# From layer 1 to layer 2 of a fused attention and two-layer MoE kernel: order of the last choice of expert, block 0's rows, ranks and the third block

## The chip, the cores and the metric

One NeuronCore of a Trainium2 chip runs the whole program. The metric is device time in microseconds, the median over runs; lower is better. Engines are named as the profile names them: PE (TensorE, matmul), DVE (VectorE), ACT (ScalarE), POOL (GpSimd) and SP (SyncE, which issues most transfers).

## The reference

Pooled attention over 8 x 8 heads feeds two mixture-of-experts layers on 4608 tokens of width 512, with 8 experts of hidden width 1024, one expert a token. Layer 2 leaves a token as it is unless its skip score is positive.

```python
# layer 1
e_idx = np.argmax(x @ w_gate + modality_bias[modality_id], axis=1)
for e in range(8):
    m = e_idx == e
    out[m] = gate_w[m, None] * (np.maximum(x[m] @ w1[e], 0) @ w2[e])
# layer 2, on layer 1's output x
do = x @ w_skip > 0
e2 = np.argmax(x[do] @ w_gate2, axis=1)
...
out[do] = x[do] + y
```

## The kernel before, in words

**Blocks.** Each layer sorts its tokens by expert into blocks of 256 slots (two tiles of 128). A block is gathered by row number into `xg` (two buffers, by the block's parity), transposed on PE (`xT`), split into a high and a low half (`xh`, `xl`), multiplied with `w1` in eight steps (`gemm1`, line 1388), and each tile then with `w2` in eight steps of three matmuls (`gemm2`, line 1448). Every product is three matmuls: high by high, high by low, low by high. `hh` and `hl` are the halves of the hidden layer; `split_w1` and `split_w2` make the weights' halves (ACT the high, DVE or POOL the low one).

**Routing of layer 2** runs beside layer 1. For every block that layer 1 has finished, DVE makes the logits (line 1728), and `picks` (line 1647) makes two steps on POOL: `first` (lines 1659 to 1674; with one maximum on DVE, `rt_mx`) and `second` (lines 1676 to 1689; with one maximum on DVE, `rt_my`), which ends with the running counts `rti`, the block's write to DRAM (`x2s`, through SP) and a scatter to the output. `rank` (line 1700) then counts with two matmuls R (lines 1707 and 1708) each token's place among its expert's: R goes to a PSUM slot with the tag `m`, of which there is one and which the routing's other counts use too; DVE reads R (`rt_rk`, line 1712). `route_places` writes four tables `OB` on POOL.

**The way over.** How many blocks layer 1 has is known only at run time; `rec` (line 1974) branches, and behind its last block runs `first2(n)` (line 1593). Block 0 of layer 2 has been gathered early, into the buffer of parity `n % 2`, and its first product runs as `gemm1(n, f)`. `epilogue2` (line 1631) adds block 0's rows from `xg[0]`; for an odd `n` they are gathered once more, into `xg[0]`. Each `gather` is two DMAs on POOL's queue, one a tile. Here `n` is 19. `first2` issues its gathers ahead of its loop; in the loop the last block's `first` and `second` come at steps 2 and 4, the rank of the block before at step 6, and the last rank at step 1 of block 0's `gemm2`, where `route` (line 1777) is begun at step 2.

**Background.** `route` is a queue of generators. Every step of `gemm2`, and in `second` twice every step of `gemm1`, calls `tick`, which runs `pace` of their steps (lines 673 to 680). The route's last steps write `gidx` (line 1046), the row numbers of all blocks of layer 2.

**Block 1.** `Layer.second` (line 1782) runs block 1's `gemm1` and first `gemm2`, then flushes the route, gathers block 2, and gives block 2's `w1` halves and transposes out over block 1's second `gemm2`. PSUM slots: three for `gemm1`, two for `gemm2`, two with the tag `tp` for transposes (`ps_t`, line 1357), one `m`.

An engine takes its instructions in program order, so an instruction that waits holds up all behind it on that engine.

Of the kernel before, what the change touches and what calls it, by code (L numbers as in the profile page):

```python
# [24 lines left out]
E = 8  # L25
# [681 lines left out]
T = 256  # L707
# [463 lines left out]
class Moe:  # L1171
# [421 lines left out]
    def first2(self, n):  # L1593

        nc, g = self.nc, self.g
        ranks = self.ranks
        self.ranks = []
        todo = [x for x in self.todo[:-11]]
        first, second = self.picks(n - 1)
        self.todo = []  # L1600
        nc.vector.tensor_copy(self.gate0, self.gate[n % 2])
        if n % 2:
            self.gather(g.r2.gidx0, 0, 0, g.x2s[0:16 * T, :])
        self.gather(g.r2.gidx0, 2, 1, g.x2s[0:16 * T, :])
        late = self.late_logits(n - 1)
        for f in range(8):
            self.gemm1(n, f)
            for x in todo[2 * f:2 * f + 2 if f < 7 else None]:
                x[2]()
            if f in (0, 2):  # L1610
                next(late)
            if f == 2:
                first()
            if f > 1:
                self.split_w2(f - 2)
            if f == 4:
                second()
            if f == 6:
                self.rank_all(ranks)
        for f in range(6, 8):  # L1620
            self.split_w2(f)
        self.gates1(1, self.sp)
        self.gemm2(0, 0, self.epilogue2, {1: self.rank_all, 2: self.L2.route,
                                          3: lambda: self.xT(1, 0, self.ps_t("ps_x")),
                                          5: lambda: self.xT(1, 1, self.ps_t("ps_x"))})
        self.gates2(1, self.sp)
        self.gemm2(0, 1, self.epilogue2)
        self.scatter(n - 1, 1)
        self.L2.second()

    def epilogue2(self, i, t, ps):
        nc, g = self.nc, self.g
# [11 lines left out]
            out=self.out, out_offset=bass.IndirectOffsetOnAxis(ap=si, axis=0), in_=o,  # L1644
            in_offset=None, bounds_check=NT - 1, oob_is_err=False)

    def picks(self, i):

        nc, g = self.nc, self.g
        P, V = nc.gpsimd, nc.vector  # L1650
# [25 lines left out]
        def second():  # L1676
            eq, val = st["eq"], st["val"]
            my = tile("rt_my")
            V.tensor_reduce(out=my, in_=eq, axis=AX.X, op=ALU.max)
            P.tensor_tensor(eq, eq, bc(my), ALU.subtract)  # L1680
            P.tensor_scalar(M, eq, 0.0, None, ALU.is_ge)
            P.tensor_tensor(M, M, bc(val), ALU.mult)
            for c in range(2):
                P.tensor_tensor(r2.carry, r2.carry, M[:, c, :], ALU.add)
                P.tensor_copy(I[:, c, :], r2.carry)
            nc.sync.dma_start(
                out=g.x2s[T * i:T * i + T, :].rearrange("(t p) w -> p t w", t=2), in_=x2)
            self.scatter(i, 0)
            self.ranks.append(i)

        return first, second

    def scatter(self, i, t):
        self.nc.gpsimd.indirect_dma_start(  # L1694
# [5 lines left out]
    def rank(self, i):  # L1700

        nc, g, r2 = self.nc, self.g, self.g.r2
        V = nc.vector
        M, I = r2.M[:, 2 * i:2 * i + 2, :], self.rti[i % 2]
        B = r2.BB[:, 2 * i:2 * i + 2]
        R = self.pp.tile([128, 2, E], F32, tag="m", name="R")
        nc.tensor.matmul(R, lhsT=g.trim, rhs=M, start=True, stop=False)
        nc.tensor.matmul(R, lhsT=g.ones, rhs=I, start=False, stop=True)
        rk = self.sp.tile([128, 2, E], F32, tag="rt_rk", name="rt_rk")
        ra = self.sp.tile([128, 2], F32, tag="rt_ra", name="rt_ra")  # L1710
        ri = self.sp.tile([128, 2], I32, tag="rt_ri", name="rt_ri")
        V.tensor_tensor(rk, M, R, ALU.mult)
        V.tensor_reduce(out=ra, in_=rk, axis=AX.X, op=ALU.add)
        V.tensor_copy(ri, ra)
        V.tensor_scalar(ri, ri, 127, None, ALU.bitwise_and)
        V.tensor_copy(B, ri)
        nc.gpsimd.tensor_tensor(r2.RH[:, 2 * i:2 * i + 2], ra, B, ALU.subtract)
        for _ in route_places(self.tc, g, r2, 2 * i, 2, nc.gpsimd):
            pass
# [33 lines left out]
class Layer:  # L1753
# [28 lines left out]
    def second(self):  # L1782

        m, g = self.m, self.m.g
        tc, r = m.tc, self.r
        bg = g.bg
        for f in range(8):
            m.gemm1(1, f)
# [2 lines left out]
        m.gemm2(1, 0, self.epilogue)  # L1791
        bg.flush()
        self.gather(2)
        if self.n == 1:
            self.gather(3)
        if self.n == 2:
            m.nc.vector.tensor_scalar(g.empty, r.tokf, BIG - 1.5, BIG, ALU.is_gt, ALU.mult)
        self.load_regs(2)
        self.load_w1(2)
        self.load_w2(2)  # L1800
        if self.n == 1:
            m.load_split(2)
            m.split_w1_if(range(8))
            m.drip(7)
        else:
            for f in range(4):
                m.split_w1(f, m.nc.gpsimd if f == 3 else None)

        def next_x(t):
            m.xT(2, t, m.ps_t("ps_x"))  # L1810
            if self.n == 2:
                m.split_w1(4 + 2 * t)
                m.split_w1(5 + 2 * t, m.nc.gpsimd)

        m.gemm2(1, 1, self.epilogue, {3: lambda: next_x(0), 5: lambda: next_x(1),
                                      6: lambda: m.gates1(2, m.sp)})
        m.gates2(2, m.sp)
        if self.n == 1:
            m.drip(5)

    def body(self, i):
        m = self.m
# [220 lines left out]
```

## Time and profile before

| | |
|---|---|
| median of 3 runs | 971.68 us (969.25 to 972.96) |
| profiled execution | 972.93 us |
| its span | 971.2 us, mean granted clock 0.964 |
| PE busy | 908.2 us (94%) |
| DVE busy | 694.7 us (72%) |
| POOL busy | 518.1 us (53%) |
| ACT busy | 372.0 us (38%) |

All times of the trace count from the start of the span. A share of busy time is an average over stages; what a stage costs is read from the gaps of PE in it and from what ended each. "Granted clock" is the share of PE's full 2.4 GHz: 1.00, or 0.50 for 1.2 GHz; a stretch that holds both shows a value between. Matmul rows overlap: the start of one to the start of the next is what one costs.

### The profile page before, as it was taken

How to read it: one execution, taken by the hardware profiler on the slowest of the kernel's cores; microseconds unless marked ns; L12 is line 12 of the kernel's file. 1: busy time of each engine (PE TensorE's matmuls, PEld its weight loads, DVE VectorE, ACT ScalarE, POOL GpSimd, SP SyncE). 2: the span in 40 equal slices, each digit the busy share in tenths (PEclk: the TensorE clock that was granted, in tenths of full speed). 3: DMA queues.
4: the chain of work that ended last, by engine and by line, in shares of the span. 5: the costliest groups of instructions: out<-in, count | busy, mean ns of one | idle time of the engine just before them, and what ended most of it. 6: DMA issues, size and time to landing. Idle time of an engine off the chain costs nothing. (4 is left out here: it accounts for less than half of the span.)

```text
span 971.2 us, 19083 instructions
## 1 busy us (share of the span) xinstructions
PE 908.2 (94%) x6205; PEld 813.5 (84%) x6205; DVE 694.7 (72%) x1843; ACT 372.0 (38%) x733; POOL 518.1 (53%) x765
## 2 busy tenths in 40 slices
PE   6899999899999999998999989999598999999994
PEld 5798898888899999987999879979586988878983
DVE  4376786776787788889777897868574667567564
ACT  2465565544122222251222512213212556565454
POOL 4745698303246647666765566565543444444443
PEclk7799999999999999999999999999988999999998
DMA  9997975523211211431224412237203764571341
GB/s 229 223 250 215 243 203 165 160 83 95 84 65 57 94 37 64 145 145 64 83 78 151 153 66 71 72 92 240 80 36 100 237 217 143 183 251 35 114 150 41
DMA packets 87386, 126.57 MB, mean 130 GB/s; under 512 B 14361, under 2 KB 51225, under 8 KB 87115
## 3 DMA queue, kind: packets, MB, share of 16 engines
q1 hardware_dynamic: 75386, 96.68, 32.7%
q0 software_dynamic: 10640, 28.12, 9.3%
q8 instruction: 62, 1.02, 0.4%
q14 instruction: 82, 0.66, 0.2%
q10 hardware_dynamic: 1216, 0.08, 0.1%
HBM read 184.72 MB, written 39.50 MB: 231 GB/s over the span
## 5 line engine op out<-in xcount | busy, mean ns | idle before, releaser
L1402 PE MATMUL ps_g<-xh,w1h 128*128 128x256 f32 x896 | 256.6, 286 | 2.3 <-DVE hl L1407 1.6
L1402 PE MATMUL ps_g<-xl,w1h 128*128 128x256 f32 x896 | 253.9, 283 | 2.6 <-DVE xl L1354 2.6
L1402 PE MATMUL ps_g<-xh,w1l 128*128 128x256 f32 x896 | 253.2, 283 | 0.0
L1728 DVE CUSTOM_DVE_ANT_0 junk<-x,W 128x512 bf16<-128x512 f32 x333 | 234.5, 704 | 19.5 <-DVEq L1332 6.2
L1455 PE MATMUL ps_g<-w2h,hh 128*128 128x512 f32 x464 | 193.6, 417 | 1.0 <-DVE rs_v L1043 0.5
L1455 PE MATMUL ps_g<-w2h,hl 128*128 128x512 f32 x464 | 186.8, 403 | 6.1 <-DVE hl L1407 6.1
L1455 PE MATMUL ps_g<-w2l,hh 128*128 128x512 f32 x464 | 186.1, 401 | 0.0
L1402 PEld LDWEIGHTS ps_g<-xh,w1h 128*128 128x128 f32 x896 | 169.9, 190 | 8.4 <-DVE hl L1407 2.0
L1402 PEld LDWEIGHTS ps_g<-xl,w1h 128*128 128x128 f32 x896 | 169.5, 189 | 4.6 <-DVE xl L1354 3.6
L1402 PEld LDWEIGHTS ps_g<-xh,w1l 128*128 128x128 f32 x896 | 169.5, 189 | 0.0
L1406 ACT ACTIVATE hh<-ps_g 128x512 fp32r<-128x512 f32 (+1 forms) x116 | 67.6, 583 | 249.5 <-PE ps_g L1402 247.1
L906 POOL TENSOR_SCALAR OB<-iota,BB,pay 128x128 bf16<-128x128 bf16 x126 | 111.9, 896 | 22.8 <-DVE BB L894 18.8
L1407 DVE SCALAR_TENSOR_TENSOR hl<-ps_g,hh 128x512 fp32r<-128x512 f32 (+1 forms) x116 | 77.6, 669 | 57.6 <-ACT hh L1406 37.9
L1455 PEld LDWEIGHTS ps_g<-w2h,hl 128*128 128x128 f32 x464 | 89.1, 192 | 30.1 <-DVE hl L1407 7.6
L1455 PEld LDWEIGHTS ps_g<-w2h,hh 128*128 128x128 f32 x464 | 89.5, 193 | 19.6 <-ACT hh L1424 1.8
L1455 PEld LDWEIGHTS ps_g<-w2l,hh 128*128 128x128 f32 x464 | 89.8, 194 | 16.9
L1322 POOL TENSOR_TENSOR w1l<-w1r,w1h 128x512 fp32r<-128x512 f32 x40 | 51.6, 1309 | 61.8 <-ACT w1h L1321 61.5
L1344 DVE TENSOR_TENSOR w2l<-w2r,w2h 128x512 fp32r<-128x512 f32 x112 | 75.2, 709 | 8.8 <-ACT w2h L1343 5.7
L1694 POOL DMA_INDIRECT out_dram<-x,dsi x38 | 47.2, 1242 | 48.1 <-DMA out_dram<-x,dsi 13.4
L1321 ACT CAST w1h<-w1r 128x512 fp32r<-128x512 f32 x120 | 68.3, 619 | 0.5 <-ACT hh L1406 0.5
L1343 ACT CAST w2h<-w2r 128x512 fp32r<-128x512 f32 x112 | 63.9, 616 | 4.1 <-DVE gidxf L1046 2.5
L1643 POOL DMA_INDIRECT out_dram<-o,o2i x21 | 25.6, 1217 | 74.7 <-DVE o2i L1642 30.7
(291 smaller groups left out, 1422.9 us busy)
## 6 DMA issues: line engine op xcount, KB each, us to landing
w1r<-in_moe_w_dram SPq DMA_DIRECT2D x128, 512.0 KB
w2r<-in_moe_w_dram SPq DMA_DIRECT2D x128, 512.0 KB
x2s<-x SPq DMA_DIRECT2D x19, 522.0 KB
v<-in_v_dram SPq DMA_DIRECT2D x48, 192.0 KB
xd<-x SPq DMA_DIRECT2D x16, 520.0 KB
q_sb<-in_q_dram SPq DMA_DIRECT2D x16, 512.0 KB
kt<-in_k_dram SPq DMA_DIRECT2D x32, 144.0 KB
x2s<-OBx SPq DMA_DIRECT2D x16, 261.0 KB
```

What stands on the lines that cost most here:

```text
L906: e.tensor_scalar(g.ob(c)[:, i, :], g.iota, r.BB[:, c:c + 1], r.pay[:, i, c:c + 1], ALU.is_equal, ALU.mult)
L1321: self.nc.scalar.copy(self.w1h[f], raw)
L1322: (eng or self.nc.vector).tensor_tensor(self.w1l[f], raw, self.w1h[f].bitcast(F32), ALU.subtract)
L1343: self.nc.scalar.copy(self.w2h[f], raw)
L1344: (eng or self.nc.vector).tensor_tensor(self.w2l[f], raw, self.w2h[f].bitcast(F32), ALU.subtract)
L1402: nc.tensor.matmul(out, lhsT=a[f][:, k, :], rhs=b[:, k, :], start=(n == 0), stop=(n == 11))
L1406: nc.scalar.activation(out=hh, in_=whole, func=ACTF.Relu)
L1407: nc.vector.scalar_tensor_tensor(hl, in0=whole, scalar=0.0, in1=hh.bitcast(F32), op0=ALU.max, op1=ALU.subtract)
L1455: nc.tensor.matmul(ps, lhsT=a[f][:, tt], rhs=b[f], start=(n == 0), stop=(n == 23))
L1643: nc.gpsimd.indirect_dma_start(out=self.out, out_offset=bass.IndirectOffsetOnAxis(ap=si, axis=0), in_=o, in_offset=None, bounds_check=NT - ...
L1694: self.nc.gpsimd.indirect_dma_start(out=self.out, out_offset=bass.IndirectOffsetOnAxis(ap=self.dsi[i % 2][:, t:t + 1], axis=0), in_=self.x ...
L1728: self.nc.vector.tensor_tensor_reduce(out=self.junk, in0=self.x2[i % 2][:, t, 0:DM], in1=self.W9[:, e, :], scale=1.0, scalar=0.0, op0=ALU. ...
```

## The change

- `picks` can give a third part, `third` (write to `x2s`, scatter, note for the rank). In `first2` the gathers ahead of the loop go: the one of block 0 is replaced by a copy on ACT at step 1, the one of block 1 stands at step 4, between `second` and `third`.
- In block 0's first `gemm2` the background's pace is 3 instead of 2, block 1's transposes stand at steps 4 and 6 instead of 3 and 5, and `gates1` of block 1 at step 7 instead of ahead of the product.
- `rank` puts R into a transposes' slot (`tp`, two of them) instead of `m`, in every block.
- Layer 2's block 1 runs in a function of its own, `second2`: it gathers block 2 as soon as the route is done, within block 1's `gemm1`; the `w1` halves stand at steps 4 to 7 of the first `gemm2`, the transposes at steps 1 and 3 of the second.

```diff
--- before.py
+++ after.py
@@ -1596,12 +1596,9 @@
         ranks = self.ranks
         self.ranks = []
         todo = [x for x in self.todo[:-11]]
-        first, second = self.picks(n - 1)
+        first, second, third = self.picks(n - 1, False)
         self.todo = []
         nc.vector.tensor_copy(self.gate0, self.gate[n % 2])
-        if n % 2:
-            self.gather(g.r2.gidx0, 0, 0, g.x2s[0:16 * T, :])
-        self.gather(g.r2.gidx0, 2, 1, g.x2s[0:16 * T, :])
         late = self.late_logits(n - 1)
         for f in range(8):
             self.gemm1(n, f)
@@ -1609,24 +1606,29 @@
                 x[2]()
             if f in (0, 2):
                 next(late)
+            if f == 1 and n % 2:
+                nc.scalar.copy(self.xg[0], self.xg[1])
             if f == 2:
                 first()
             if f > 1:
                 self.split_w2(f - 2)
             if f == 4:
                 second()
+                self.gather(g.r2.gidx0, 2, 1, g.x2s[0:16 * T, :])
+                third()
             if f == 6:
                 self.rank_all(ranks)
         for f in range(6, 8):
             self.split_w2(f)
-        self.gates1(1, self.sp)
+        g.bg.pace = 3
         self.gemm2(0, 0, self.epilogue2, {1: self.rank_all, 2: self.L2.route,
-                                          3: lambda: self.xT(1, 0, self.ps_t("ps_x")),
-                                          5: lambda: self.xT(1, 1, self.ps_t("ps_x"))})
+                                          4: lambda: self.xT(1, 0, self.ps_t("ps_x")),
+                                          6: lambda: self.xT(1, 1, self.ps_t("ps_x")),
+                                          7: lambda: self.gates1(1, self.sp)})
         self.gates2(1, self.sp)
         self.gemm2(0, 1, self.epilogue2)
         self.scatter(n - 1, 1)
-        self.L2.second()
+        self.L2.second2()
 
     def epilogue2(self, i, t, ps):
         nc, g = self.nc, self.g
@@ -1644,7 +1646,7 @@
             out=self.out, out_offset=bass.IndirectOffsetOnAxis(ap=si, axis=0), in_=o,
             in_offset=None, bounds_check=NT - 1, oob_is_err=False)
 
-    def picks(self, i):
+    def picks(self, i, whole=True):
 
         nc, g = self.nc, self.g
         P, V = nc.gpsimd, nc.vector
@@ -1683,12 +1685,16 @@
             for c in range(2):
                 P.tensor_tensor(r2.carry, r2.carry, M[:, c, :], ALU.add)
                 P.tensor_copy(I[:, c, :], r2.carry)
+            if whole:
+                third()
+
+        def third():
             nc.sync.dma_start(
                 out=g.x2s[T * i:T * i + T, :].rearrange("(t p) w -> p t w", t=2), in_=x2)
             self.scatter(i, 0)
             self.ranks.append(i)
 
-        return first, second
+        return (first, second) if whole else (first, second, third)
 
     def scatter(self, i, t):
         self.nc.gpsimd.indirect_dma_start(
@@ -1703,7 +1709,7 @@
         V = nc.vector
         M, I = r2.M[:, 2 * i:2 * i + 2, :], self.rti[i % 2]
         B = r2.BB[:, 2 * i:2 * i + 2]
-        R = self.pp.tile([128, 2, E], F32, tag="m", name="R")
+        R = self.ps_t("R2")[:, 0, 0:2 * E].rearrange("p (c e) -> p c e", e=E)
         nc.tensor.matmul(R, lhsT=g.trim, rhs=M, start=True, stop=False)
         nc.tensor.matmul(R, lhsT=g.ones, rhs=I, start=False, stop=True)
         rk = self.sp.tile([128, 2, E], F32, tag="rt_rk", name="rt_rk")
@@ -1782,7 +1788,6 @@
     def second(self):
 
         m, g = self.m, self.m.g
-        tc, r = m.tc, self.r
         bg = g.bg
         for f in range(8):
             m.gemm1(1, f)
@@ -1791,32 +1796,57 @@
         m.gemm2(1, 0, self.epilogue)
         bg.flush()
         self.gather(2)
-        if self.n == 1:
-            self.gather(3)
-        if self.n == 2:
-            m.nc.vector.tensor_scalar(g.empty, r.tokf, BIG - 1.5, BIG, ALU.is_gt, ALU.mult)
+        self.gather(3)
         self.load_regs(2)
         self.load_w1(2)
         self.load_w2(2)
-        if self.n == 1:
-            m.load_split(2)
-            m.split_w1_if(range(8))
-            m.drip(7)
-        else:
-            for f in range(4):
-                m.split_w1(f, m.nc.gpsimd if f == 3 else None)
+        m.load_split(2)
+        m.split_w1_if(range(8))
+        m.drip(7)
+        m.gemm2(1, 1, self.epilogue, {3: lambda: m.xT(2, 0, m.ps_t("ps_x")),
+                                      5: lambda: m.xT(2, 1, m.ps_t("ps_x")),
+                                      6: lambda: m.gates1(2, m.sp)})
+        m.gates2(2, m.sp)
+        m.drip(5)
+
+    def second2(self):
+
+        m, g = self.m, self.m.g
+        r, bg, pool = self.r, g.bg, m.nc.gpsimd
+        ready = []
+
+        def begin():
+            if ready or bg.q:
+                return
+            ready.append(True)
+            self.gather(2)
+            self.load_regs(2)
+            self.load_w1(2)
+            self.load_w2(2)
+            m.nc.vector.tensor_scalar(g.empty, r.tokf, BIG - 1.5, BIG, ALU.is_gt, ALU.mult)
+
+        for f in range(8):
+            m.gemm1(1, f)
+            bg.tick()
+            bg.tick()
+            begin()
+        bg.flush()
+        begin()
+        bg.pace = 2
+
+        def split(f):
+            return lambda: m.split_w1(f, pool if f in (3, 7) else None)
+
+        m.gemm2(1, 0, self.epilogue, {4 + f: split(f) for f in range(4)})
 
         def next_x(t):
             m.xT(2, t, m.ps_t("ps_x"))
-            if self.n == 2:
-                m.split_w1(4 + 2 * t)
-                m.split_w1(5 + 2 * t, m.nc.gpsimd)
-
-        m.gemm2(1, 1, self.epilogue, {3: lambda: next_x(0), 5: lambda: next_x(1),
-                                      6: lambda: m.gates1(2, m.sp)})
+            split(4 + 2 * t)()
+            split(5 + 2 * t)()
+
+        m.gemm2(1, 1, self.epilogue, {1: lambda: next_x(0), 3: lambda: next_x(1),
+                                      5: lambda: m.gates1(2, m.sp)})
         m.gates2(2, m.sp)
-        if self.n == 1:
-            m.drip(5)
 
     def body(self, i):
         m = self.m
```

## Rows read from the trace of the kernel before

**Rows 1.** Timeline of PE around both gaps: start, us, engine, line, out<-in, count [idle<-releaser].
```profile
694.12 0.39 PE L1455 MATMUL ps_g<-w2l,hh 128*128 128x512 f32 x1
694.36 0.39 PE L1455 MATMUL ps_g<-w2h,hl 128*128 128x512 f32 x1
...
703.23 0.19 PE L1707 MATMUL R<-M,trim 128*128 128x16 bf16 x1 [8.48 <-DVE rt_rk L1712]
703.99 0.17 PE L1708 MATMUL R<-rti,ones 128*128 128x16 bf16 x1 [0.57 <-POOL rti L1685]
...
744.49 0.90 PE L1350 MATMUL ps_x<-ident,xg 128*128 128x128 f32 x3 [3.92 <-DMA xg<-x2s,gidx]
```

**Rows 2.** Timeline of VectorE (DVE), 689 to 703, around the last choice of expert.
```profile
689.94 0.16 DVE L1590 COPY lg<-ps_lg 128x9 f32<-128x9 f32 x1
...
701.10 0.17 DVE L1679 TENSOR_REDUCE rt_my<-rt_eq 128x2 f32<-128x16 f32 x1 [8.40 <-POOL rt_eq L1673]
...
701.78 1.30 DVE L1344 TENSOR_TENSOR w2l<-w2r,w2h 128x512 fp32r<-128x512 f32 x2
```

**Rows 3.** Timeline of GpSimd (POOL), 692 to 707: gathers, choice, scatter.
```profile
692.30 1.33 POOL L1314 DMA_INDIRECT xg<-x2s,gidxf  x1 [3.62 <-DMA out_dram<-x,dsi]
...
698.44 0.20 POOL L1663 COPY x<-lg 128x18 f32<-128x18 f32 x1
...
700.85 0.22 POOL L1673 TENSOR_TENSOR rt_eq<-rt_eq,desc 128x16 f32<-128x16 f32 x1
...
701.98 0.56 POOL L1682 TENSOR_TENSOR M<-M,d_val 128x16 bf16<-128x16 bf16 x1
...
703.74 0.19 POOL L1685 CAST rti<-carry 128x8 bf16<-128x8 f32 x1
705.82 1.56 POOL L1694 DMA_INDIRECT out_dram<-x,dsi  x1 [1.88 <-DMA xg<-x2s,gi]
```

**Rows 4.** Table by stretches: us, busy us of each engine, PEclk, DMA share, GB/s.
```profile
694.70:704.00 9.30, 0.25 (x3) 0.15 (x3) 2.76 (x10) 0.90 (x2) 6.48 (x20) 0.75 0.51 163
704.00:709.60 5.60, 5.60 (x16) 4.53 (x16) 4.65 (x13) 0.80 (x2) 3.75 (x5) 0.50 0.12 46
709.60:740.60 31.00, 30.97 (x273) 27.11 (x272) 18.63 (x65) 5.04 (x9) 8.84 (x12) 1.00 0.06 20
740.60:744.50 3.90, 0.01 (x1) 0.02 (x1) 0.00 (x0) 0.00 (x0) 3.23 (x3) 0.90 0.95 309
744.50:750.60 6.10, 6.10 (x19) 5.02 (x20) 2.22 (x4) 3.17 (x6) 1.34 (x1) 0.51 0.44 140
```

**Rows 5.** Timelines of DVE and POOL, 733 to 742: the third block's gather.
```profile
733.71 0.19 DVE L1046 TENSOR_SCALAR gidx<-rs_v 128x52 int32<-128x52 f32 x1
...
738.92 1.27 POOL L1643 DMA_INDIRECT out_dram<-o,o2i  x1 [15.23 <-DVE empty L1797]
740.49 1.06 POOL L1314 DMA_INDIRECT xg<-x2s,gidx  x1 [0.30 <-issue]
```

**Rows 6.** DMA issues of the whole span: transfer, queue, count, median us to landing.
```profile
xg<-x2s,gidx POOLq DMA_INDIRECT x22, 3.9
...
xg<-x2s,gidxf POOLq DMA_INDIRECT x4, 3.4
```

**Rows 7.** Timeline of ScalarE (ACT): a copy of 512 columns.
```profile
682.01 0.59 ACT L1584 COPY o<-ps_x 128x512 f32<-128x512 f32 x1 [2.48 <-issue]
```

**Rows 8.** Timelines of PE and DVE in layer 1's block 17 and the next.
```profile
636.90 0.18 PE L1707 MATMUL R<-M,trim 128*128 128x16 bf16 x1 [1.32 <-DVE rs_v L1043]
...
651.06 0.17 DVE L1679 TENSOR_REDUCE rt_my<-rt_eq 128x2 f32<-128x16 f32 x1 [4.04 <-POOL rt_eq L1673]
...
654.17 0.38 PE L1402 MATMUL ps_g<-xh,w1h 128*128 128x256 f32 x1 [0.61 <-ACTq L1332]
```

**Rows 9.** Timelines of DVE and PE in layer 1's tightest block: rank and transposes.
```profile
567.21 0.17 DVE L1712 TENSOR_TENSOR rt_rk<-M,R 128x16 f32<-128x16 bf16 x1
...
569.18 0.64 PE L1350 MATMUL ps_x<-ident,xg 128*128 128x128 f32 x4
```

## The prediction

> **What bounds the kernel now.** TensorE (PE) has work for almost the whole span, so I read its idle time, not its share. I took the timeline of PE first, looking for gaps; then, for each gap, the engine named as releaser, back to the instruction that was late; then the table by stretches, for what the clock did after each gap; last the transfers' times to landing. The reader is to see two gaps on the way from layer 1 to layer 2, and one small one before.
>
> Gap A: PE stops after the second step of block 0's second product (694.6) and stands until 703.99, because the matmuls R of `rank` for the last block of layer 1 wait: first for VectorE's `rt_rk`, which must read the one PSUM slot that R is to overwrite, then for POOL's `rti` [rows 1]. VectorE is not busy; its queue stands behind `rt_my`, 8.40 us idle for POOL [rows 2]. POOL had the logits at 690.1 [rows 2], but ran four gathers, 692.30 to 698.44, ahead of the choice of expert [rows 3]. Idle: 8.48 + 0.57 = 9.05 us. The granted clock is then 0.50 (the 1.2 GHz level) for 5.6 us of full work [rows 4]: 2.8 us more. Gap A costs 11.85 us.
>
> Gap B: the transposes of block 2 wait 3.92 us for its gather [rows 1]. The row numbers `gidx` were ready at 733.9, but the gather is issued at 740.49, behind block 1's scatter [rows 5]. Clock again: 6.1 us at 0.51 [rows 4], 3.0 us lost. Together 6.9 us.
>
> **The change, part by part.** All is summed against the profiled execution, 972.93 us, which is 1.25 us above the median of the three runs shown; the difference is then taken off that median.
>
> *Choice ahead of gathers.* POOL's first step after its branch becomes `first()`. It can't start before 690.1 (logits). From the other side: the first gather starts at 692.30, and a DMA on POOL starts 1.9 us after the work ahead of it (703.93 to 705.82) [rows 3], so the branch was over near 690.4, which I take. `first()` took 2.63 us (698.44 to 701.07) with VectorE idle. Now it runs beside the subtractions of `split_w2(0)` to `(2)`. One POOL step beside such a pair [rows 2] took 0.56 us where its like took 0.22 [rows 3]; some three steps lose 0.34 each, 1.0 us (between 0 and 2.0, the length of three subtractions). So `first()` ends at 694.0, `rt_my` follows by 694.25, and POOL's second part, 2.66 us (701.27 to 703.93, beside the same subtractions as before), ends at 696.9. R no longer waits for `rt_rk` (it has two slots now), only for `rti`: PE, there at 694.6, waits 2.3 us, between 1.3 and 3.3, not 9.05.
>
> The Trainium skill, "SBUF — State Buffer", section "Who interferes with whom", speaks against this move: a VectorE instruction with two SBUF inputs and a GpSimd instruction that reads SBUF exclude each other, and the later one waits out the whole of the other. By that rule the delay would be the 2.0 us, and the sum 1.0 us worse; the row's 0.34 per step shows the delay but less than a whole instruction.
>
> *Block 1's gathers* now follow `second()`: start 696.9 + 1.9 = 698.8, landing 3.4 us later [rows 6], 702.2; the second about 1.5 us later (four in 6.14 us). PE meanwhile does three steps of three matmuls, 0.24 us apart [rows 1], and is at the transposes (now at step 4) at 699.1: a new wait of 3.1 us. As both hang on `rti`, it stays near 3.1 whatever `rti` does; with the 3.9 us of the other gathers it is 3.6. For the second transposes (step 6) PE comes at 704.0 and the rows at 703.7: nothing. Queued behind the gathers on POOL are block 18's scatter, the ranks' `RH` and eight `OB` tables; they come earlier than before, since two gathers are gone. `gates1`, now at step 7, no longer makes VectorE wait for rows; moved past it, ranks and route only gain.
>
> *Clock.* Idle of 2.3 and 3.1 us stands where 9.05 was. Idle of 3.92 us cost 3.0, so the bounds are 0 and 3.0. A low clock behind the first wait is free, as PE then waits for the gather anyway; behind the second it costs. I take 1.7, a little over half. Gap A afterwards: 2.3 + 3.1 + 1.7 = 7.1; gain 4.7 us (between 1.9: 3.3 + 3.6 + 3.0 left; and 7.4: 1.3 + 3.1 left).
>
> *Copy of block 0's rows.* 2 x 522 columns at the price of a 512-column copy, 0.59 us [rows 7], are 1.2 us on ScalarE, between two activations for which it waits on PE. Nothing, covered by that idle time; without it 1.2 us, on `w2h` for VectorE. The issue that it replaces (two gathers, 3 us of POOL) is counted above.
>
> *Third block sooner.* In the code the route takes 60 steps. Two a tick, they end in block 1's second product; three a tick, 15 fit behind step 2 of block 0's first half, 24 into its second half, and the last 21 into four of block 1's eight `gemm1`. The gather is then issued some 10 us of PE work before its transposes, against 3.9 needed [rows 6]: gap B goes, 6.9 us (3.9 if the clock falls all the same). SP's weight loads are released by block 2's splits, which only come earlier. What is late next: VectorE, which must do the route in less time. It is busy 18.6 of 31 us there [rows 4]; losing some 9 us of that stretch leaves 18.6 in 22. PE's counting matmuls use tables made three rounds earlier, so I take 0, and 1.5 us as the other end.
>
> *Ranks in the transposes' slots*, in every block of layer 1. It frees PE of 1.32 us at 636.90, where R waited for another user of the old slot. But that block's end hangs on POOL: `rt_my` at 651.06 waits 4.04 us for it, and PE waits for what comes behind at 654.17 [rows 8]. Between 0 and 1.3; I take 0.3. The price is a new wait: the second transposes of a block now need the rank's slot read. In the tightest block `rt_rk` ends at 567.38 and those transposes start at 569.18 [rows 9]: covered by 1.8 us.
>
> Sum: 4.7 + 6.9 + 0.3 = 11.9 us, 972.93 to 961.0; off the median, 971.68 to **959.8 us**.
>
> **Rivals.** (1) *Gap A only changes its name*: contention at its worst, a slow landing and a low clock through the block put the wait for `rti` and rows where the old one was. For it: both new waits hang on one POOL chain. Against: two gathers leave that chain. Only gap B is won: 971.68 - 6.9 = 964.8. (2) *VectorE becomes the bound*: the denser route delays the tables, the transposes' low halves, and PE stops in block 1 instead. For: some 85% busy by my estimate above. Against: three rounds of lead. Gap A's gain alone, 967.0. (3) *Slower*: the shared slots stop PE in layer 1. If in the 17 later blocks VectorE's rank came later than now, each block would pay what exceeds 1.8 us; from 0.7 us a block (11.9 / 17) the gain is gone, and a rank 4 us later costs 2.2 x 17 = 37 us: 997. For it: the tight block is real. Against: nothing in the change delays ranks there, and where the rank is late PE already waits for `hl`, which VectorE makes just behind it. (4) *It does not do what it says*: the copy replaces gathers only for an odd block count; the four gathers before the choice are that case, so I leave this out. (5) Gains and new waits cancel, about 971.
>
> **How the numbers follow.** Forecast 0.72, (1) 0.16, (2) 0.06, (5) 0.03, (3) 0.03. The forecast's own bounds: at best 1.3 + 7.4 + 6.9 = 15.6, 956.1; at worst 0 + 1.9 + 3.9 - 1.5 = 4.3, 967.4, with all ends at once. The spread of the runs of before (969.25 to 972.96) adds half a us below. The range, 955.5 to 966.0, takes in (1) and leaves out (2), (3), (5) and the forecast's far corner. Half a per cent, 4.9 us, is about what a measurement of this kernel can tell from no change: faster than 966.8 are the forecast, (1) and part of (2), 0.88; within it 0.09; slower 0.03.
>
> **What would show it.** Right: R behind 694.6 waits under 3.5 us, and for POOL's `rti` alone; the first transposes of block 1 wait about 3 us for DMA; no PE gap before block 2's transposes, and the granted clock at 1.00 there; block 2's gather is issued inside block 1's `gemm1`. Wrong: a wait for VectorE in block 1's `gemm1`; transposes in layer 1 that wait for `rt_rk`; R waiting over 5 us; a clock of 0.50 for 5 us or more after gap A.

## The result and the profile after

The changed kernel takes **963.28 us** (median of 5 runs, 962.16 to 967.72); the kernel before, run beside it, 972.17 us (5 runs, 969.25 to 973.79). The ratio is 0.9905, interval [0.9886, 0.9924]: 9.2 us faster, between 7.4 and 11.1. Forecast: 959.8, inside 955.5 to 966.0. The sign was right, and both gaps changed as forecast; the sum, 11.9 us, was 2.7 us too large. The profiled execution is the slowest of the five, 967.72 us (span 966.0), so the two profiles are compared over a stretch of equal work, not over their spans.

That stretch runs from the first product of layer 2's block 0 to block 2's first product, the same 425 matmuls in both. Table by stretches, kernel before (us, busy us of each engine, PEclk, DMA share, GB/s; blocks 0 and 1):

```profile
678.60:717.40 38.80, 28.36 (x171) 24.70 (x170) 24.90 (x79) 9.06 (x17) 23.95 (x42) 0.87 0.20 64
717.40:751.10 33.70, 29.78 (x257) 26.10 (x256) 15.46 (x45) 7.70 (x14) 8.26 (x8) 0.90 0.24 78
sum 72.50, PE 58.14 PEld 50.81 DVE 40.36 ACT 16.76 POOL 32.21; mean PE 29.07 PEld 25.40 DVE 20.18 ACT 8.38 POOL 16.11
```

The same table, changed kernel:

```profile
682.40:719.70 37.30, 29.61 (x182) 25.78 (x182) 27.34 (x85) 10.81 (x20) 23.88 (x43) 0.91 0.18 61
719.70:747.20 27.50, 26.35 (x245) 23.62 (x245) 16.43 (x45) 7.92 (x15) 7.94 (x7) 1.00 0.31 100
sum 64.80, PE 55.96 PEld 49.40 DVE 43.77 ACT 18.73 POOL 31.82; mean PE 27.98 PEld 24.70 DVE 21.89 ACT 9.37 POOL 15.91
```

72.5 became 64.8: **7.7 us**. PE's idle time is sum less busy, 14.36 before and 8.84 after. The rest is clock: PE worked 11.8 us at 0.50 before and 6.8 us after, half of which is loss, 5.9 and 3.4. Both tell 8.0 us; the 0.3 us that are left over are matmuls that take a little longer at full clock.

The gaps one by one. Timeline of PE, changed kernel, answering to [rows 1] (start, us, engine, line, out<-in, count, [idle<-releaser]):

```profile
695.48 0.39 PE L1402 MATMUL ps_g<-xh,w1h 128*128 128x256 f32 x1 [2.88 <-DVE hl L1407]
...
702.51 0.17 PE L1714 MATMUL R<-rti,ones 128*128 128x16 bf16 x1 [0.84 <-POOL rti L1687]
...
706.22 0.17 PE L918 MATMUL R<-rc_cb,ones 128*128 128x8 bf16 x1 [1.34 <-DVE rc_cb L914]
708.27 0.66 PE L1350 MATMUL ps_x<-ident,xg 128*128 128x128 f32 x4 [1.89 <-DMA xg<-x2s,gidxf]
...
718.68 0.47 PE L1156 MATMUL W<-rs_oa,OB 128*128 128x52 bf16 x12 [0.74 <-DVE rs_oa L1148]
...
747.20 0.36 PE L1402 MATMUL ps_g<-xh,w1h 128*128 128x256 f32 x1 [1.15 <-DVE o2i L1644]
```

The 9.05 us for `rt_rk` and `rti` are 0.84; in their place stand 1.34 + 1.89 = 3.23 us before block 1's transposes (a small matmul of the route stands first, waits for DVE's `rc_cb` and delays nothing, as the rows come later still). The 3.92 us before block 2's transposes are gone. Two waits are new: 0.74 for `rs_oa`, an operand of the route's counting matmuls, and 1.15 at block 2's first product. The wait for `hl` ahead of step 6 of block 0's `gemm1` grew from 1.40 to 2.88.

Table by stretches, changed kernel, answering to [rows 4]: from step 6 to R, and from block 1's transposes on.

```profile
695.40:701.60 6.20, 6.12 (x33) 5.59 (x34) 4.65 (x12) 1.24 (x3) 4.86 (x14) 0.72 0.23 86
708.20:713.50 5.30, 5.23 (x20) 4.32 (x21) 2.76 (x10) 1.17 (x2) 5.27 (x9) 0.68 0.28 90
```

A clock of 0.72 over 6.20 us is 3.4 us at the 1.2 GHz level, 0.68 over 5.30 as well: after each of the two waits PE works 3.4 us at half speed and loses half of it.

Timeline of POOL, changed kernel, answering to [rows 3]:

```profile
695.62 0.74 POOL L1665 COPY x<-lg 128x18 f32<-128x18 f32 x1 [2.70 <-DVE lg L1590]
...
696.91 0.65 POOL L1668 TENSOR_TENSOR d_val<-d_pos,tokf 128x2 f32<-128x2 f32 x1
697.62 0.52 POOL L1669 CAST dsi<-d_val 128x2 int32<-128x2 f32 x1
...
699.36 0.22 POOL L1675 TENSOR_TENSOR rt_eq<-rt_eq,desc 128x16 f32<-128x16 f32 x1
...
702.27 0.19 POOL L1687 CAST rti<-carry 128x8 bf16<-128x8 f32 x1
704.37 1.56 POOL L1314 DMA_INDIRECT xg<-x2s,gidxf  x1 [1.91 <-DMA out_dram<-x,dsi]
...
730.29 1.06 POOL L1314 DMA_INDIRECT xg<-x2s,gidx  x1 [3.13 <-DVE rs_lo L1165]
```

The choice begins as soon as the logits are there. Its first part takes 695.62 to 699.58, 3.96 us (2.63 in [rows 3]), and it ends at 702.46; the gather starts 1.91 us behind it. Block 2's gather, at 730.29, stands in the sixth step of block 1's `gemm1` and 10.5 us ahead of its transposes (740.81).

Timeline of VectorE, changed kernel: the last logits (answering to [rows 2]), then the three subtractions of `split_w2` that run beside the choice's first part.

```profile
695.34 0.15 DVE L1590 COPY lg<-ps_lg 128x9 f32<-128x9 f32 x1
695.62 0.69 DVE L1344 TENSOR_TENSOR w2l<-w2r,w2h 128x512 fp32r<-128x512 f32 x1
...
696.82 0.68 DVE L1344 TENSOR_TENSOR w2l<-w2r,w2h 128x512 fp32r<-128x512 f32 x1
697.42 0.68 DVE L1344 TENSOR_TENSOR w2l<-w2r,w2h 128x512 fp32r<-128x512 f32 x1
```

Counted from block 0's first product (678.64 before, 682.46 in the changed kernel) the logits are ready 11.46 us behind it before and 13.03 after.

Timeline of ScalarE, changed kernel: the copy that replaces block 0's two gathers.

```profile
686.88 1.06 ACT L1610 COPY xg<-xg 128x1044 f32<-128x1044 f32 x1
```

### The profile page after: what moved, and what is told of

Same layout as the page of the kernel before. It is cut to its first block, busy times and chain, and to the rows that moved or that the text cites. A ratio compares the mean times of both kernels' runs of the same rounds, so it can differ in the third digit from the quotient of the medians.

```text
span 966.0 us, 19093 instructions
## 1 busy us (share of the span) xinstructions
PE 908.6 (94%) x6205; PEld 813.6 (84%) x6205; DVE 696.9 (72%) x1844; ACT 373.2 (39%) x734; POOL 517.6 (54%) x762
## 5 line engine op out<-in xcount | busy, mean ns | idle before, releaser
L368 PE MATMUL ps_av<-VB,et 96*128 96x146 f32 (+1 forms) x480 | 64.5, 288 | 0.0
```

The lines of the kernel that those rows point to most:

```text
L368: nc.tensor.matmul(ps[p0:p1, j // 3, o:o + 2 * VW], lhsT=t[:, j, p0:p1], rhs=VB[b % NR][:, j].rearrange("p i w -> p (i w)"), start=(j % 3 ...
```

## The experiments

Gains are 1 less the ratio, times 972 us. "Stretch" is the stretch above, from one profile each: 72.5 before, 64.7 in the changed kernel. A place such as "11.5 us behind" counts from block 0's first product in that run's own trace.

**The changed kernel once more** (`after_again`, no edit).

> The changed kernel once more, to tell what belongs to it from what one execution drew. Theory: three waits in its profile are its own: 0.8 us for the choice, 1.3 + 1.9 us at block 1's transposes, 1.15 us ahead of block 2's first product; they come again within 0.3 us. The 2.88 us ahead of step 6 of layer 2's first product (1.40 in the kernel before) and the 3.4 us more of low clock in layer 1 are chance and differ this time: time 963 us, between 962 and 964.5. Rival: the 2.88 us is the change's own (VectorE comes later to the branch), it comes again between 2.5 and 3.2 us with a low clock behind it.

963.63 us (961.29 to 966.48), ratio 0.9911 [0.9891, 0.9931]; stretch 64.9 with the same six gaps: 2.62, 0.84, 1.36, 1.91, 1.04, 1.18 us and no other. The new waits come again in a second execution. So does the one ahead of step 6, 2.62 us with 3.4 us of low clock behind it, as the rival said; but in `pace2` and `static_third` below, the same program up to that step, it is 1.32 and 1.42, and in `no_third` 1.87. The edits up to there do not force it, and what does is open.

**The third block alone** (`third_only`): the kernel before with `second2`, nothing else.

```diff
         self.scatter(n - 1, 1)
-        self.L2.second()
+        self.L2.second2()
```

> The kernel before with block 1's new function alone: gathers ahead of the choice, ranks in the old slot, pace 2. Theory: gap A stays at 9 us with a clock of 0.50 for some 5.6 us; gap B goes with its low clock (6.9 us), but about 1.2 us comes ahead of block 2's first product, because the branch and the loads of its registers stand in PE's program there and are hidden only while the array lags behind its sequencer; net 5.7 us less than before, 966.5 us. Rival 1: that wait is for VectorE's work at the end of block 1, made dense by the new order; here the route is not denser, so it shrinks under 0.5 us and the gain is 6.5 us or more. Rival 2: the clock falls all the same; gain under 4 us.

968.71 us (963.15 to 970.01), ratio 0.9959 [0.9942, 0.9977]: 4.0 us, between 2.2 and 5.6. Timeline of PE:

```profile
699.28 0.19 PE L1707 MATMUL R<-M,trim 128*128 128x16 bf16 x1 [7.62 <-DVE rt_rk L1712]
...
736.50 0.66 PE L1350 MATMUL ps_x<-ident,xg 128*128 128x128 f32 x4 [0.19 <-DMA xg<-x2s,gidx]
...
742.32 0.36 PE L1402 MATMUL ps_g<-xh,w1h 128*128 128x256 f32 x1 [2.35 <-issue]
```

Gap A stands and gap B is gone, as in the edit. But the 6.9 us booked for gap B aren't all there: 2.35 us come back at block 2's first product. That wait hangs on nothing in the profile ("issue"; the queue of PE, shown further down, tells more); the theory had 1.2 us there. The profiled execution took 964.23 us, 4.5 us under the median of its twelve runs, so its rows (stretch 5.3 us shorter) show more than the median's 4.0.

**All but the third block** (`no_third`): the changed kernel with the old `second()`.

```diff
-        self.L2.second2()
+        self.L2.second()
```

> The changed kernel with layer 2's block 1 as it was before: the route still runs at pace 3 in block 0's first product, the choice is still ahead of the gathers. Theory: gap A shrinks as in the changed kernel (waits of 0.8, 1.3 and 1.9 us and some 1.7 us of low clock), gap B is there again, about 4 us with about 3 us of low clock behind it, and no wait ahead of block 2's first product: 968.5 us, some 3.5 us under before. Rival: the two parts help each other (the earlier route also frees gap B), then gap B is under 3 us and the time is under 967.

970.12 us (967.65 to 972.91), ratio 0.9985 [0.9970, 1.0001]: 1.5 us, from nothing to 2.9. Timeline of PE:

```profile
743.00 0.86 PE L1350 MATMUL ps_x<-ident,xg 128*128 128x128 f32 x4 [4.10 <-DMA xg<-x2s,gidx]
...
749.83 0.36 PE L1402 MATMUL ps_g<-xh,w1h 128*128 128x256 f32 x1 [1.35 <-DVE g_mx L1372]
```

Gap B is back, and behind it, here too and against the theory, a wait before block 2's first product. The two halves gain 4.0 + 1.5 = 5.5 us, the whole 9.2. In the profiles they nearly add up (stretch shorter by 5.3 and 1.7 against 7.7); with intervals of 1.5 us or more on each median, what is left of the difference stays open.

**Ranks back in their own slot** (`ranks_m`).

```diff
-        R = self.ps_t("R2")[:, 0, 0:2 * E].rearrange("p (c e) -> p c e", e=E)
+        R = self.pp.tile([128, 2, E], F32, tag="m", name="R")
```

> The changed kernel with R back in the one slot m. Theory: the slot is worth next to nothing once the choice is early. In the profile of the changed kernel the rank ahead had been read at 701.7, and the last choice ended at 702.5: R waits for the choice either way. Block 17 of layer 1 has its 1.3 us ahead of R again, but the wait for the low halves behind it shrinks by as much: time within 0.7 us of the changed kernel, 963 to 964. Rival: the slot is what freed PE; then R waits 2 us or more for rt_rk and the time is over 965.

962.79 us (960.83 to 965.94), ratio 0.9904 [0.9885, 0.9923]: the slots are worth nothing that shows. Timeline of PE:

```profile
637.81 0.18 PE L1713 MATMUL R<-M,trim 128*128 128x16 bf16 x1 [1.33 <-DVE rs_lo L1041]
...
698.24 0.18 PE L1713 MATMUL R<-M,trim 128*128 128x16 bf16 x1 [1.61 <-DVE rt_rk L1718]
699.00 0.17 PE L1714 MATMUL R<-rti,ones 128*128 128x16 bf16 x1 [0.58 <-POOL rti L1687]
```

Both waits for the slot are back, and neither shows in the time. Block 17 of layer 1, where the first stands, takes 27.78 us in the kernel before and 28.30 here, both with that wait; in the two profiles of the changed kernel, without it, 27.65 and 28.07. Behind the second, R waits 0.58 us more for `rti` in any case.

**Order or number of gathers?** Two kernels. `gather_first`: the changed kernel with block 1's two gathers ahead of the loop, as before, and the copy ahead of them. `four_first`: block 0's two as well, in place of the copy (the diff).

```diff
         nc.vector.tensor_copy(self.gate0, self.gate[n % 2])
+        if n % 2:
+            self.gather(g.r2.gidx0, 0, 0, g.x2s[0:16 * T, :])
+        self.gather(g.r2.gidx0, 2, 1, g.x2s[0:16 * T, :])
...
-            if f == 1 and n % 2:
-                nc.scalar.copy(self.xg[0], self.xg[1])
...
-                self.gather(g.r2.gidx0, 2, 1, g.x2s[0:16 * T, :])
```

> The changed kernel with block 1's two gathers ahead of the loop again (the copy of block 0's rows stands before them). Theory: what helped is that two of four gathers are gone, not the order: in either order one POOL chain of choice and two gathers (3.4 us) ends ahead of block 1's transposes. R waits for the choice some 3.5 us longer (over 4 us in all), the transposes wait for no rows; the counting matmul still waits for the ranks: time within 2 us of the changed kernel, 963 to 965.5. Rival: the order is the point, R's wait grows to 6 us or more with a low clock of two stretches behind it, and the time is over 966.

> The changed kernel with all four gathers ahead of block 0's loop and no copy on ScalarE, as in the kernel before; the rest of the change stays. It differs from the run with two gathers ahead (gather_first, 961.0 us, R waiting 4.37 + 1.22 us for POOL, 6.8 us of low clock) by two gathers alone. Theory A, the two dropped gathers are what shortens gap A: two more gathers at the 3.4 us that POOL took for the like put R's wait at about 8 to 9 us with some 10 us of low clock behind it, and the time at 964 to 967 us. Theory B, the gain comes from the third block alone and gap A's share is noise: R waits longer, but the time stays at 961 to 963 us, as for gather_first.

`gather_first`: 961.0 us (959.08 to 963.83), ratio 0.9900 [0.9879, 0.9921]. `four_first`: 965.45 us (963.86 to 968.25), 0.9934 [0.9916, 0.9952]. Timeline of PE, `gather_first`:

```profile
695.63 0.17 PE L1713 MATMUL R<-M,trim 128*128 128x16 bf16 x1 [4.37 <-POOL M L1684]
697.02 0.17 PE L1714 MATMUL R<-rti,ones 128*128 128x16 bf16 x1 [1.22 <-POOL rti L1687]
```

and `four_first`:

```profile
699.22 0.17 PE L1713 MATMUL R<-M,trim 128*128 128x16 bf16 x1 [7.72 <-POOL M L1684]
700.61 0.17 PE L1714 MATMUL R<-rti,ones 128*128 128x16 bf16 x1 [1.22 <-POOL rti L1687]
```

`gather_first` is 2 us faster than its theory had it. The move itself gains nothing that shows in the time; with 2 us either way on each ratio, a gain or loss of some 2 us would not. Gathers first, R waits 5.59 us and the rows are there; choice first, R waits 0.84 and the rows are late by 3.23, with a low clock either way (stretch 64.7 in both). These two profiles are not quite alike: the logits stand 13.0 us behind block 0's first product in the changed kernel and 11.5 in `gather_first`. With logits as early as that (`pace2` and `static_third` below) the kernels with the choice first have block 1's transposes 24.3 to 24.4 us behind, `gather_first` 26.0. So by the rows the order is worth some 1.7 us, less than the low clock gave or took from one kernel to the next (0 to 6.8 us at 0.50 behind the transposes' wait).

The two gathers that the copy spares are worth 3.35 us of R's wait, 3.1 of the stretch, and 3.3 of the time by the ratios (some 2.8 either way).

**Pace 2 instead of 3** in block 0's products (`pace2`).

```diff
-        g.bg.pace = 3
```

> The changed kernel with the background at pace 2 in block 0's products. Theory: the faster route is not needed for the third block; the gather is issued at the end of block 1's first product, still ahead of its transposes, so that gap B stays away; and the wait of 0.7 to 1.0 us for the counting tables goes, as does the wait of 1.3 us for the ranks ahead of the transposes, though that only lengthens the wait for the rows behind it: time 962 to 963.5, the same or up to 1 us less. Rival: without pace 3 the gather comes too late, PE waits 2 us or more at block 2's transposes, time over 965.

962.82 us (961.91 to 965.25), ratio 0.9915 [0.9896, 0.9934]: no difference. The wait for `rs_oa` goes, and block 2's gather, at the end of block 1's `gemm1`, is still early enough. Timeline of PE:

```profile
701.83 1.09 PE L1350 MATMUL ps_x<-ident,xg 128*128 128x128 f32 x4 [3.57 <-DMA xg<-x2s,gidxf]
...
742.57 0.36 PE L1402 MATMUL ps_g<-xh,w1h 128*128 128x256 f32 x1 [2.23 <-DVE gate L1386]
```

What the denser pace cost (0.74 to 1.04) it gave back at block 2's first product, 1.15 instead of 2.23.

**The first three subtractions of `split_w2` behind the choice** (`split_after`).

```diff
-            if f > 1:
-                self.split_w2(f - 2)
             if f == 4:
                 second()
...
+                for j in range(3):
+                    self.split_w2(j)
+            if f > 4:
+                self.split_w2(f - 2)
```

> The changed kernel with VectorE's and ScalarE's halves of w2 0 to 2 behind the second part of the choice instead of beside the first. Theory: the first part takes 4.0 us in the changed kernel against 2.6 before because POOL's steps stand still beside VectorE's subtractions of two tiles in SBUF; without them it takes 2.6 to 2.8 again, and the choice ends about 1.3 us earlier. The time hardly moves, as the low halves are then late for block 0's product: 962.5 to 965. Rival: the 1.3 us are a matter of the branch just passed (first instructions fetched late), and the first part takes 3.5 us or more again.

963.22 us (959.39 to 965.2), ratio 0.9912 [0.9890, 0.9935]. Timeline of POOL, the same three steps as above:

```profile
690.14 0.20 POOL L1667 COPY x<-lg 128x18 f32<-128x18 f32 x1 [2.27 <-DVE lg L1590]
...
690.88 0.20 POOL L1670 TENSOR_TENSOR d_val<-d_pos,tokf 128x2 f32<-128x2 f32 x1
691.15 0.19 POOL L1671 CAST dsi<-d_val 128x2 int32<-128x2 f32 x1
...
693.74 0.56 POOL L1685 TENSOR_SCALAR M<-rt_eq 128x16 bf16<-128x16 f32 x1
```

With these subtractions gone from beside it, 0.74, 0.65 and 0.52 us are 0.20, 0.20 and 0.19, and the part takes 2.63 us instead of 3.96. The contention is real, 1.33 us, and the rival of the branch just passed is out. Most of it only moves: the second part, now beside the subtractions, takes 3.6 instead of 2.6, and from the logits to `rti` it is 6.6 instead of 7.0.

The rows of the changed kernel show how it works. Each slow step of POOL starts while a subtraction runs and ends some 0.05 us behind that subtraction's end: 696.36 behind 696.30, 697.56 behind 697.50, 698.15 behind 698.10.

**Block 1's transposes in block 0's second half** (`x_late`), ranks and route two and four steps later; and with it (`x_late_pace2`, the diff) pace 2 and the route at step 4.

```diff
-        g.bg.pace = 3
-        self.gemm2(0, 0, self.epilogue2, {1: self.rank_all, 2: self.L2.route,
-                                          4: lambda: self.xT(1, 0, self.ps_t("ps_x")),
-                                          6: lambda: self.xT(1, 1, self.ps_t("ps_x")),
-                                          7: lambda: self.gates1(1, self.sp)})
+        self.gemm2(0, 0, self.epilogue2, {3: self.rank_all, 4: self.L2.route})
+        self.gemm2(0, 1, self.epilogue2, {2: lambda: self.xT(1, 0, self.ps_t("ps_x")),
+                                          4: lambda: self.xT(1, 1, self.ps_t("ps_x")),
+                                          6: lambda: self.gates1(1, self.sp)})
         self.gates2(1, self.sp)
-        self.gemm2(0, 1, self.epilogue2)
```

> The changed kernel with the last rank at step 3 and the route at step 6 of block 0's first half, and block 1's transposes at steps 2 and 4 of its second half, gates at 6. Theory: PE's waits for the choice, the ranks and the rows (0.8 + 1.3 + 1.9 us) exist only because PE is asked for them before POOL can have them; put behind six more steps they go, with the low clock behind them (1.7 us): the gap between the end of step 1 and the transposes is under 1 us in all, time 958 to 960. Rival: the work was moved, not won: VectorE then has ranks, low halves and route in a shorter stretch, PE waits for the transposes' low halves or the counting tables instead, over 2 us, time 961.5 or more.

> The run with block 1's transposes in the second half (x_late, 958.6 us) with the route at two steps a tick instead of three and begun at step 4 instead of 6. Theory A, of the waits left in x_late the one for the loads' operand in block 1's first products (1.1 us) is VectorE crowded by the denser route: it goes, and the time falls to 957.5. Theory B, what VectorE no longer does early it does late: the wait ahead of block 2's first product grows by as much, or its gather comes late, and the time is 958.6 to 959.5.

`x_late`: 958.61 us (955.97 to 960.31), ratio 0.9869 [0.9848, 0.9890]. `x_late_pace2`: **955.68 us** (954.87 to 957.46), ratio 0.9829 [0.9813, 0.9845], the fastest: 16.6 us under the kernel before. The table by stretches of `x_late_pace2`:

```profile
677.70:706.00 28.30, 26.30 (x170) 22.52 (x169) 21.69 (x65) 9.81 (x17) 18.50 (x35) 1.00 0.18 60
706.00:735.00 29.00, 26.98 (x257) 23.93 (x256) 21.04 (x63) 8.14 (x16) 12.83 (x13) 1.00 0.34 108
```

and its timeline of PE:

```profile
695.66 0.17 PE L1712 MATMUL R<-rti,ones 128*128 128x16 bf16 x1 [0.71 <-POOL rti L1685]
699.37 0.17 PE L918 MATMUL R<-rc_cb,ones 128*128 128x8 bf16 x1 [0.33 <-DVE rc_cb L914]
...
735.01 0.36 PE L1402 MATMUL ps_g<-xh,w1h 128*128 128x256 f32 x1 [2.03 <-DVE gate L1386]
```

The rows were never late as such: their transposes were too early. With other work of PE ahead of them the 3.23 us shrink to 0.33 (in `x_late` 0.56, for the rows), the granted clock stays at 1.00 throughout (3.4 us more), and the stretch is 57.3 us. Against `pace2`, its neighbour in pace, `x_late_pace2` gains 8.4 us by the ratios. From `x_late` to it the ratios tell 3.9 us (some 2.6 either way), more than theory A had: the waits of 1.11 us for `rs_oa` and 0.59 for `xl` are gone, and block 2's first product waits 2.03 instead of 1.58.

**Block 2 without the run-time branch ahead of it** (`static_third`, and `x_late_static` on top of the two edits of `x_late_pace2`; the expectation of the latter sets it against `x_late`, but the kernel holds the pace edit too, so its neighbour is `x_late_pace2`). It leaves out the run-time test whether layer 2 has a third block (here it has), so it is a measurement and no version to keep.

```diff
-        L2 = Layer(self, 2, r2, g.x2s, 0, self.epilogue2)
+        L2 = Layer(self, 2, r2, g.x2s, 3, self.epilogue2)
```

> The changed kernel with block 2 treated as a block that always runs, so that the branch on the number of blocks and its register stand behind block 2 instead of ahead of it; the number of rows is still loaded. Theory A, the 1.2 to 2.4 us that PE stands ahead of block 2's first product are its own register loads and branch: the stretch from the last product of block 1 to the first of block 2 shrinks by 0.3 to 0.8 us, and the time by as much (962.5 to 963). Theory B, it is VectorE's last work on block 1's output, for which PE would wait in any case: unchanged, 963.3.

> The two edits together: block 1's transposes in the second half, and block 2 without the run-time branch ahead of it. If the register loads and the branch end the wait ahead of block 2's first product: 0.3 to 0.8 us under x_late's 958.6, so 957.8 to 958.3. If not: 958.6.

962.14 us (959.57 to 964.58), ratio 0.9899 [0.9878, 0.9919], and 955.98 us (953.34 to 956.52), 0.9822 [0.9805, 0.9839]: by time neither can be told from its neighbour. The profiled execution of `static_third` is the shortest of its six. By the rows the wait shrinks from 1.15 to 0.82 us and from 2.03 to 0.76, and what is left is the sequencer's own work. The queue of PE, changed kernel (line, instruction, count, shortest/median/longest in ns, first and last start):

```profile
L2011 PEldq COMPARE_BRANCH  x2: 77/1706/3335, 742.4 to 746.2; - x2
L2022 PEldq TENSOR_LOAD <-nb x1: 305/305/305, 745.7 to 745.7; - x1
L1950 PEldq TENSOR_LOAD <-full x1: 296/296/296, 746.3 to 746.3; - x1
```

`static_third`, which has the second load alone (the longer branch stays there, 3.48 us from 734.05):

```profile
L1950 PEldq TENSOR_LOAD <-full x1: 297/297/297, 737.6 to 737.6; - x1
```

`x_late_pace2`:

```profile
L2009 PEldq COMPARE_BRANCH  x2: 77/1996/3915, 729.6 to 734.0; - x2
```

and the kernel before:

```profile
L1981 PEldq COMPARE_BRANCH  x2: 77/1926/3775, 745.8 to 750.1; - x2
L1992 PEldq TENSOR_LOAD <-nb x1: 305/305/305, 749.6 to 749.6; - x1
```

Timeline of PE, `x_late_static`:

```profile
735.37 0.36 PE L1402 MATMUL ps_g<-xh,w1h 128*128 128x256 f32 x1 [0.76 <-ACT gd L1380]
```

The releaser that the profile prints for this wait (`o2i`, `gate`, `gd`, "issue") differs from kernel to kernel; the load of `full` stands in it every time, that of `nb` in all but `static_third` and `x_late_static`, and ahead of them a branch of `rec` (`tc.If(self.nb > i)`, line 2011 in the changed kernel, 2009 and 1981 in the other two). In the changed kernel the branch begins at 742.35, 3.3 us ahead of block 1's last matmul (745.66), and ends at 745.69; `nb` is loaded at once, and from the last weights (745.61) to the first weights of block 2 (747.17) it is 1.56 us. In `third_only`, `pace2` and `x_late_pace2`, all of pace 2, `nb` is loaded 1.0 to 1.3 us after the last weights. It is the branch that stands there: it begins only 2.8 to 3.0 us ahead of the last matmul and takes 3.9 to 4.1 us. In the kernel before it took 3.8 us as well, but began 5.0 us ahead of the last matmul (745.75 and 750.75). Why a branch takes PE's queue 3.3 to 4.1 us no run shows.

## Why the prediction was right, and where it was not

*Gap A, choice ahead of gathers.* The chain was right, its start was not. From the logits (695.49) to `rti` (702.46) it is 6.97 us, predicted 6.8; the gather's 1.91 us are the 1.9 that was taken; the rows are late by 3.23 us, predicted 3.1. But the sum took the logits where the kernel before had them, 11.46 us behind block 0's first product, and in the two profiles of the changed kernel they stand 13.03 and 12.84 behind. The rows then landed 3.9 us after their issue, not 3.4. With both and the 0.2 of the chain, block 1's transposes stand 2.2 us later than the sum had them. R waits 0.84 and not 2.3, since PE came 3.2 us later than taken (1.5 more at step 6, 1.7 of low clock behind it) and `rti` 1.7 us later. In `static_third` and `pace2`, where the logits come at 11.5 and 11.4, R waits 2.2 us, close to the 2.3.

VectorE is late in the changed kernel before its branch is reached: an `rt_my` in layer 1's last block stands 0.68 us behind block 0's first product, in `pace2` 0.65 us ahead of it. What makes it late is open; no edit stands between the two programs up to there.

Gap A with the wait at step 6 and the low clock went from 13.25 us (1.40 + 9.05 + 2.8) to 10.35 (2.88 + 0.84 + 3.23 + 3.4), a gain of 2.9, not 4.7.

*A low clock behind the first wait is free.* This held. R waits 2.2 us in `static_third` and in `pace2`. Behind it 3.4 us at 0.50 follow in the one; in the other the clock falls only in the last 0.7 us, while PE waits for rows already. From R to the transposes it is 5.85 and 5.93 us all the same. Tables by stretches from R to the transposes, `static_third`, then `pace2`:

```profile
694.67:700.52 5.85, 3.82 (x12) 2.53 (x11) 3.52 (x10) 0.00 (x0) 3.11 (x3) 0.71 0.27 56
695.90:701.83 5.93, 2.36 (x11) 1.65 (x10) 3.52 (x10) 0.00 (x0) 3.19 (x3) 0.94 0.24 56
```

The low clock behind step 6 in the changed kernel is of the same kind: with it the transposes stand 12.8 us behind the logits, in `pace2`, without it, 12.9.

*The clock behind the second wait* cost 1.7 us, as taken, and that was luck: behind like waits it was 3.4 in `pace2` (6.8 us at 0.50) and nothing in `static_third`.

*Order or number.* The sum has the order and the two spared gathers in one term. The gathers' share shows by itself (`four_first` against `gather_first`, 3.3 us); the order's does not show in the time. Rival 1, that gap A only changes its name, was right about the move. About the whole the time alone does not decide (`no_third` gains 1.5 us, from nothing to 2.9); the rows, with 2.9 us, speak against it.

*Contention on POOL.* Estimated at 1.0 us, measured 1.33. The rule of the Trainium skill ("SBUF — State Buffer", "Who interferes with whom") is borne out by the rows: the three slow steps stand still until the subtraction beside them has ended. The 2.0 us that the prediction put down to that rule were too much: a step that starts during a subtraction (0.68 to 0.69 us) loses only what is left of it less its own 0.2 us, here 0.54, 0.45 and 0.33 us.

*Copy.* 1.06 us on ScalarE (predicted 1.2). Two instructions later ScalarE waits 1.36 us for PE, so the copy delays nothing.

*Third block, gap B.* 3.92 us idle and 3.0 of clock are gone, as forecast. The gather came 10.5 us ahead of its transposes, "some 10", though in the sixth step of block 1's `gemm1` and not behind the fourth. The step that failed is "what is late next", answered with VectorE alone. What was late next was PE's own queue. In the kernel before, PE ran its last products of block 1 at 0.50 until 750.5 [rows 4], its sequencer was 5.0 us ahead of the array when it came to the branch, and branch and loads ended beside those products, unseen. At full clock it is 3.3 us ahead, and the array stands idle for 1.15 us. `no_third` fits: the same code as before, but PE works 3.4 us instead of 6.0 at 0.50 behind gap B, and there the wait is 1.35.

*VectorE crowded.* Taken at 0 with 1.5 as the other end: 0.74 us for `rs_oa` here, 0.5 to 1.8 in the kernels of pace 3, none at pace 2.

*Slots.* Taken at 0.3. In block 17 the wait of 1.32 us is gone, and the block is 0.1 us shorter (27.78 and 27.65); no time shows it.

The account over the stretch, in which block 17 does not lie: 2.9 (gap A) + 6.9 (gap B) - 0.7 (`rs_oa`) - 1.15 (branch and loads) - 0.3 (matmuls at full clock) = 7.65, against 7.7 measured. The median of the runs moved by 9.2 (7.4 to 11.1); the rest lies within its interval.

## What to carry to other kernels

When an engine's queue holds back a result, count what can leave the queue before changing its order: the same work in another order moved the wait from R to the rows and gained nothing that shows in the time, while two spared gathers gained some 3 us. A consumer that arrives early is mended by moving the consumer, here by six steps of a product for some 7 us. When a gap closes, look at what lay in its shadow: branches and register loads that a slow array hides are not in the old profile as waits. And a forecast for a chain needs the time of its first link in the new kernel: 1.6 us were lost there.

## What the runs showed that was not expected

- PE's run-time branch is bare time when its sequencer isn't far enough ahead of the array. The branch takes 3.3 to 4.1 us in PE's queue, the two register loads behind it 0.30 us each. Begun 5.0 us ahead of the last matmul it left no gap (the kernel before); 3.3 us ahead it left the array idle for 1.15 us (the changed kernel), 2.8 to 3.0 us ahead for 2.0 to 2.35 (pace 2). Without the load of `nb` and the test behind it 0.8 is left.
- The low clock follows different waits in different kernels, even where the program is the same up to there: 3.4 us at 0.50 behind the step 6 wait in the changed kernel, 3.4 behind R's in `static_third`, 6.8 behind the rows' in `pace2`. It is 6.8 behind R's in `gather_first`, 10.2 in `four_first` (half of it while R waits), and none in `x_late_pace2`, whose longest wait before block 2 is 0.92 us.
- POOL's small steps beside a subtraction of two tiles on VectorE end with that subtraction: 0.52 to 0.74 us instead of 0.19 to 0.20.
